# Local softmax of every other head pair: the shift and the sums on VectorE, one ScalarE exponential of 640 columns, and a new order table

## The chip, the core and the metric

The kernel runs on one core of a Trainium2 chip. The core has five engines that run side by side, each with its own queue of instructions in order: TensorE (PE in the profile; its weight loads are PEld), VectorE (DVE), ScalarE (ACT), GpSimd (POOL) and SyncE (SP), which issues the DMAs. The metric is the device time of one execution, in microseconds, as the median of several runs.

## What is computed

Inputs are q, k, v (4 batches, 8 heads, 576 positions, 64 columns) and the weights of two mixing layers. The first part is the one the change is about:

```python
# local attention: |i - j| < 4; 1/sqrt(64) = 0.125
scores = np.where(mask, scale * np.matmul(q, k.transpose(0, 1, 3, 2)), -1000000000.0)
scores = scores - np.max(scores, axis=-1, keepdims=True)
attn = np.exp(scores)
attn = attn / (np.sum(attn, axis=-1, keepdims=True) + 1e-09)
out = out_up + np.matmul(attn, v)     # out_up: attention over means of 4 positions
```

Then a token mixer (576 to 256 to 576 positions), a channel mixer (512 to 1536 to 512 columns, both with ReLU and a residual), and an attention layer with four experts of which each token uses two.

## The kernel before

*Units.* A unit is one pair of heads of one batch: 4 batches x 4 pairs = 16 units, numbered 0 to 15. For the local attention the 576 positions are cut into ten windows of 58 queries that see 64 keys each. A unit's scores are a PSUM tile `sl` of 128 partitions by 2 x 5 x 64 = 640 columns: two windows above each other, five pairs of windows (`t`), two heads (`h`). The mask is added by a first product of a band with an identity matrix.

*Steps of a unit.* `q` loads queries and keys, `sl` makes the scores (PE), `mx` takes the maximum over 64 keys with a minus sign into `nraw` (VectorE) and scales it by 0.125 into `nmx`, `ex` makes ten exponentials of 64 columns, each with its bias from `nmx` and with its row sum (ScalarE; the sum is read by an instruction of its own), `rs` adds 1e-9 and inverts (VectorE), `P` multiplies (GpSimd), `tl` transposes (PE), `tc` copies out of PSUM (ScalarE). The steps `qd kd sd md ed rd Pd pdt pc` do the same for the down-sampled attention, `v` and `pv` bring the values. For two units at a time `ol` multiplies with the values, `oc` copies the down-sampled part and `ad` adds both into `u` (VectorE).

*The token mixer* runs by halves of a batch: `tx` transposes, `xh` and `xl` split into a high and a low part (ScalarE, VectorE), `h` is the first product, `hh` and `hl` split its ReLU, `pu` is the second product and `ua` adds it to `u` (VectorE). *Weights* 0 to 12 come as 64-bit numbers and are turned by `w g t a f gd add hi lo` over SP, ScalarE, VectorE and GpSimd. *The channel mixer* begins with the steps `uh ul` (split of `u`), `fc` (first product), `gh gl`, `sc` (second product) and `ac`, and goes on in a loop, `ch_step`, behind the table. The expert layer follows in a second written table, which the change leaves alone.

*What sets the order.* In the attention stage the order of all steps is written out by hand in the table `STEPS`: each engine gets its instructions in the order of the words and carries them out in that order. PSUM has four single banks and two double banks there (`ABANKS`); `sl` and `sd` share the two double ones. `P` has four buffers, `nraw`, `nmx`, `sm` and `rs` three.

Of the kernel before, what the change touches and what calls it, by code (L numbers as in the profile page):

```python
# [49 lines left out]
STEPS = """  # L50
    w0 q0 g0 t0 w1 qd0 q1 g1 sl0 kd0 gd0 a0 mx0 gd1 sd0 f0 q2 ex0 add0 a1 kd1 t1 sl1 q3 md0 qd1 f1 add1 ed0 rs0 kd2
    hi0 hi1 w2 mx1 ex1 qd2 sd1 rd0 lo0 g2 md1 lo1 ed1 P0 tl0.0 sd2 tc0.0 qd3 v0 rs1 w3 t2 sl2 kd3 Pd0 P1 md2 rd1
    pdt0 g3 gd2 a2 ed2 mx2 rd2 f2 tl1.0 q4 tl0.1 v1 add2 gd3 t3 pc0 q5 sd3 ex2 tl1.1 Pd1 qd4 md3 pdt1 hi2 a3 tc0.1
    lo2 rs2 ed3 w4 rd3 pv0 q6 Pd2 tc1.0 pc1 tc1.1 sl3 g4 mx3 pv1 ex3 f3 sl4 v2 gd4 a4 t4 w5 mx4 qd5 v3 f4 rs3 ol0.0
    ol0.1 sl5 Pd3 add3 P2 kd4 P3 oc0 add4 ex4 ad0.3 ad0.0 ad0.1 pdt3 ad0.2 pc3 mx5 tx0.1 tl3.0 xh0.1 pv2 tx0.2 rs4
    tc3.0 xl0.1 q7 sd4 w6 xh0.2 hi4 hi3 tx0.0 pv3 kd5 xh0.0 tl2.0 xl0.2 md4 tl2.1 xl0.0 lo3 tl3.1 P4 tc2.0 h0.0 lo4
    qd7 ex5 g6 pdt2 pc2 h0.1 rs5 sd5 g5 gd5 ed4 gd6 a6 a5 f5 md5 tc3.1 t6 f6 sl7 tc2.1 v4 hh0 t5 ed5 ol1.0 kd7 hl0
    oc1 add5 mx7 rd4 hi5 ol1.1 ad1.0 add6 hi6 lo5 ex7 ad1.1 sl6 ad1.3 v5 pu0.0 q8 ad1.2 ua0.0 tl4.0 tx1.2 tc4.0 lo6
    xh1.2 kd6 mx6 pv5 q9 w7 P5 xl1.2 kd9 tx1.1 q10 xh1.1 pu0.1 pu0.2 Pd4 rd5 xl1.1 ua0.1 ua0.2 pu0.3 tl5.0 Pd5 ex6
    pdt4 tx1.0 xh1.0 w8 qd6 ua0.3 pv4 qd9 tc5.0 sd7 kd10 pc4 sd6 qd8 tl5.1 xl1.0 v6 kd8 rs6 md7 g7 pdt5 tl4.1 g8 pc5  # L60
    tc4.1 ed7 tc5.1 P6 t7 h1.0 gd7 h1.1 rs7 t8 v7 md6 gd8 a7 hh1 sl9 f7 hl1 ol2.0 ed6 mx9 rd7 oc2 ex9 ol2.1 q11
    ad2.0 sd9 ad2.1 pv6 pu1.0 ad2.3 w9 v8 rd6 Pd7 ad2.2 pdt7 tx2.1 sl8 pu1.1 md9 q12 ua1.0 ed9 q13 pc7 rs9 xh2.1
    qd10 q14 pu1.2 mx8 ua1.1 pv7 pu1.3 ex8 xl2.1 Pd6 a8 rd9 ua1.2 tx2.0 ua1.3 pdt6 tx2.2 xh2.0 tl6.0 pc6 sd8 xh2.2
    tc6.0 P9 f8 P7 sd10 rs8 xl2.0 tl6.1 tl7.0 xl2.2 md10 tc6.1 qd11 tc7.0 tl9.0 md8 v9 P8 qd12 qd13 tl8.0 tc9.0
    tc8.0 ed8 tl9.1 add8 tl7.1 qd14 h2.0 add7 ed10 tc9.1 tc7.1 h2.1 sl10 ol3.0 hh2 Pd9 pv8 v10 kd11 oc3 mx10 hl2 rd8
    ad3.0 hi7 ex10 pv9 Pd8 sl11 ol3.1 pu2.0 ad3.2 ad3.1 ad3.3 ua2.0 mx11 pu2.1 tx3.2 pdt8 tx3.1 xh3.2 ua2.1 xl3.2
    tx3.0 pdt9 pc8 lo7 xh3.1 xh3.0 xl3.1 tl8.1 sd11 xl3.0 ex11 kd12 pu2.2 md11 kd14 h3.0 tc8.1 pc9 rs10 g9 ua2.2
    sd12 ed11 pu2.3 P10 rs11 P11 md12 ed12 h3.1 gd9 a9 f9 rd12 hh3 ol4.0 hl3 oc4 t9 ua2.3 sl13 ad4.0 v11 ad4.1 sl12
    tl10.0 pv10 rd10 add9 tl11.0 v12 w10 tc10.0 mx12 tc11.0 q15 ol4.1 rd11 ad4.2 pu3.0 Pd10 ua3.0 pu3.1 tl11.1 ex12
    ad4.3 tx4.0 tc11.1 xh4.0 ua3.1 tx4.2 pu3.2 tx4.1 mx13 xh4.2 xl4.0 pv12 xl4.2 pdt10 tl10.1 ua3.2 hi8 xh4.1 hi9  # L70
    kd13 w11 ex13 xl4.1 lo9 rs12 lo8 pu3.3 h4.0 g10 pv11 h4.1 tc10.1 rs13 pc10 sd13 hh4 P12 ua3.3 tl12.0 hl4 Pd11
    md13 pdt11 tl12.1 g11 pc11 gd11 tc12.0 a11 pu4.0 gd10 v13 tc12.1 ua4.0 ed13 qd15 ol5.0 sl14 kd15 oc5 P13 a10
    ol5.1 ad5.0 t10 sl15 ad5.1 tl13.0 tc13.0 ad5.2 ad5.3 rd13 mx15 tx5.2 tx5.0 tx5.1 xh5.2 xh5.0 pu4.1 Pd13 xl5.2
    xl5.0 xh5.1 xl5.1 ex15 tl13.1 mx14 pu4.2 ua4.1 f10 ua4.2 tc13.1 pv13 add10 Pd12 h5.0 pu4.3 h5.1 ex14 pdt12 pdt13
    hh5 sd15 sd14 rs15 ua4.3 hl5 pu5.0 rs14 pc13 pc12 P14 ol6.0 P15 hi10 md15 f11 md14 ua5.0 oc6 ed15 pu5.1 pu5.2
    ad6.0 ad6.1 ol6.1 lo10 ua5.1 rd15 w12 v14 ua5.2 ed14 t11 ad6.3 Pd15 g12 pu5.3 tl14.0 rd14 ad6.2 tx6.2 v15 ua5.3
    Pd14 tx6.0 gd12 tc14.0 tl14.1 tx6.1 xh6.2 xh6.0 xh6.1 tc14.1 xl6.2 xl6.0 xl6.1 tl15.0 pdt14 tc15.0 pdt15 t12
    pv14 pv15 a12 tl15.1 pc15 h6.0 tc15.1 h6.1 pc14 hh6 f12 ol7.0 hl6 oc7 ol7.1 ad7.1 ad7.0 ad7.2 pu6.0 ad7.3 uh0.3
    uh0.2 ul0.2 uh0.1 ua6.0 add12 tx7.1 tx7.2 uh0.0 tx7.0 ul0.1 ul0.0 xh7.0 hi12 ul0.3 xh7.2 pu6.1 fc0.0 fc0.1 xh7.1
    gh0.0 add11 xl7.0 xl7.1 gl0.0 fc0.2 hi11 pu6.2 gh0.1 gh0.2 uh1.3 gl0.1 ua6.1 xl7.2 gl0.2 h7.0 lo11 pu6.3 uh1.0  # L80
    uh1.2 lo12 sc0.2 ul1.3 ul1.2 uh1.1 h7.1 ul1.0 uh2.1 ac0.2 sc0.3 ul1.1 ua6.2 fc1.0 ac0.3 gh1.0 gl1.0 sc0.0 hh7
    hl7 fc1.1 ac0.0 gh1.1 ul2.1 fc1.2 gl1.1 pu7.0 pu7.1 pu7.2 uh2.2 gh1.2 sc0.1 gl1.2 ua6.3 uh2.3 ul2.3 ul2.2 ua7.2
    uh2.0 ua7.1 ul2.0 pu7.3 ac0.1 ua7.0 ua7.3
"""


# [958 lines left out]
```

## Time and profile before

| | |
|---|---|
| median of 3 runs | 659.18 us (659.09 to 660.15) |
| the profiled execution | 660.12 us, span 658.3 us |
| busy: PE, PEld | 627.7, 562.6 us |
| busy: VectorE, ScalarE, GpSimd | 443.1, 378.6, 148.3 us |
| mean granted TensorE clock | 0.99 of full speed |

The span runs from the first to the last instruction. Busy time is the union of an engine's instructions; PE's products are pipelined, so a busy PE is not a PE at its peak. The attention stage takes about the first 150 us; the first channel product starts at 152.81 us.

### The profile page before, as it was taken

The numbers are of one execution on the slowest core, as the hardware profiler recorded it, in microseconds if no ns is written. First come the engines' busy times: TensorE is split into PE (matmuls) and PEld (weight loads), VectorE is DVE, ScalarE is ACT, GpSimd is POOL, SyncE is SP. The second block draws the span as 40 slices with busy tenths as digits, with TensorE's granted clock in tenths as the row PEclk, the third lists the DMA queues.
The fourth block names the chain that finished last, engine by engine and source line by source line (L and its number), as shares of the span: only waits on it lengthen the run. The fifth ranks groups of instructions, "written<-read, shape, count | busy, mean of one in ns | idle before, by whom it ended". The sixth has DMA issues, their size and how long they took to land.

```text
span 658.3 us, 13779 instructions
## 1 busy us (share of the span) xinstructions
PE 627.7 (95%) x5196; PEld 562.6 (85%) x5196; DVE 443.1 (67%) x1075; ACT 378.6 (58%) x1213; POOL 148.3 (23%) x167
## 2 busy tenths in 40 slices
PE   3888999999999999999999999999989999999996
...
DVE  7889977787688767447644545443488766858871
ACT  6988999865364544234433332320387787677782
...
DMA packets 28947, 46.78 MB, mean 71 GB/s; under 512 B 3216, under 2 KB 16016, under 8 KB 28880
## 3 DMA queue, kind: packets, MB, share of 16 engines
...
## 4 chain that ended last, share of the span: by engine, by line
PE 80%; ACT 9%; DVE 7%; DMA 2%; issue 1%; SPq 0%; ACTq 0%; DVEq 0%
PE c L218 46%; PE proj L218 7%; PE vp L218 4%; PE wo L218 4%; PE o L943 4%; ACT P L411 4%; PE pt L920 3%; PE s L881 2%; PE s L882 2%; PE pu L218 2%; ACT pd L440 2%; PE h L218 2%; DMA wt_raw<-in_wt_dram 1%; DVE u L521 1%; PE tl L468 1%
## 5 line engine op out<-in xcount | busy, mean ns | idle before, releaser
L218 PE MATMUL c<-uh,wch 128*128 128x460 f32 (+1 forms) x240 | 89.2, 372 | 0.0
L218 PE MATMUL c<-hh,wch 128*128 128x460 f32 (+1 forms) x240 | 89.2, 371 | 0.0
L218 PE MATMUL c<-hl,wch 128*128 128x460 f32 (+1 forms) x240 | 89.1, 371 | 0.0
L218 PE MATMUL c<-hh,wcl 128*128 128x460 f32 (+1 forms) x240 | 89.1, 371 | 0.0
L218 PE MATMUL c<-ul,wch 128*128 128x460 f32 (+1 forms) x240 | 89.1, 371 | 0.0
L218 PE MATMUL c<-uh,wcl 128*128 128x460 f32 (+1 forms) x240 | 88.9, 371 | 0.0
L198 ACT ACTIVATE hh<-c 128x460 fp32r<-128x460 f32 (+1 forms) x60 | 33.0, 550 | 90.4 <-PE c L218 90.1
L776 POOL TENSOR_TENSOR vlo<-u,vh 128x576 fp32r<-128x576 f32 x16 | 22.8, 1425 | 240.2 <-ACT vh L772 240.2
L207 DVE SCALAR_TENSOR_TENSOR hl<-c,hh 128x460 fp32r<-128x460 f32 (+1 forms) x60 | 38.1, 635 | 55.2 <-ACT hh L198 55.0
L280 POOL TENSOR_TENSOR wc_t<-wc_f,wc_t 128x512 int32<-128x512 int32 x24 | 31.8, 1336 | 157.6 <-ACT wc_t L269 137.8
L638 ACT ACTIVATE uh<-u 128x460 fp32r<-128x460 f32 (+1 forms) x80 | 45.3, 585 | 25.0 <-PE c L218 19.8
L644 DVE TENSOR_TENSOR ul<-u,uh 128x460 fp32r<-128x460 f32 (+1 forms) x80 | 51.9, 664 | 8.3 <-ACT uh L638 8.3
L898 ACT ACTIVATE Pc<-Pc,nm 116x116 f32<-116x116 f32 (+4 forms) x80 | 46.7, 586 | 8.1 <-DVE nm L891 6.1
L891 DVE CUSTOM_DVE_ANT_0 Pc<-s,caus 116x348 f32<-116x348 f32 (+4 forms) x80 | 40.2, 515 | 15.2 <-PE s L882 11.6
L218 PEld LDWEIGHTS c<-hh,wcl 128*128 128x128 f32 x240 | 45.1, 188 | 5.3
L218 PEld LDWEIGHTS c<-uh,wcl 128*128 128x128 f32 x240 | 45.1, 188 | 5.2
L218 PEld LDWEIGHTS c<-hh,wch 128*128 128x128 f32 x240 | 45.2, 188 | 5.1
L218 PEld LDWEIGHTS c<-ul,wch 128*128 128x128 f32 x240 | 45.1, 188 | 5.1
L218 PEld LDWEIGHTS c<-uh,wch 128*128 128x128 f32 x240 | 45.1, 188 | 5.1
L218 PEld LDWEIGHTS c<-hl,wch 128*128 128x128 f32 x240 | 45.1, 188 | 5.1
L411 ACT ACTIVATE P<-sl,nmx 128x64 f32<-128x64 f32 x160 | 47.9, 355 | 2.7 <-DVE nmx L404 2.7
L411 ACT ACTIVATION_READ_ACCUMULATOR P<-sl,nmx 128x1 f32 x160 | 38.8, 249 | 0.0
...
## 6 DMA issues: line engine op xcount, KB each, us to landing
...
```

The source lines that it names most:

```text
L198: nc.scalar.activation(hi, src, AF.Relu if relu else AF.Copy, **({"scale": scale} if scale else {}))
L207: nc.vector.scalar_tensor_tensor(lo, src, 0.0, h, op0=OP.max, op1=OP.subtract)
L218: mm(ps, a, c, start=first and i == 0, stop=last and i == n - 1)
L280: nc.gpsimd.tensor_tensor(t, r["f"], t, op=OP.add)
L411: nc.scalar.activation(P[:, t, h], r["sl"][:, h, t], AF.Exp, bias=r["nmx"][:, t, h:h + 1], scale=0.125, accum_out=sm[:, 2 * t + h:2 * t + ...
L638: nc.scalar.activation(hi, UA[:, c, blocks[k]], AF.Copy)
L644: nc.vector.tensor_tensor(lo, UA[:, c, blocks[k]], hi.bitcast(F32), op=OP.subtract)
L776: nc.gpsimd.tensor_tensor(lo, U[b][:, c], hi.bitcast(F32), op=OP.subtract)
L891: nc.vector.tensor_tensor_reduce(dst, r["s", t, e], mask, -1.0, 3.0e38, OP.add, OP.min, nm[:nq])
L898: nc.scalar.activation(P[:nq, :n], P[:nq, :n], AF.Exp, bias=r["nm", t, e][:nq], scale=-1.0, accum_out=r["su", t][:nq, e:e + 1])
L920: tp(pt[:TS[c], (c - c0) * TQ:(c - c0) * TQ + nq], P[:nq, c * TQ:c * TQ + TS[c]], ident[:nq, :nq])
L943: mm(o[64 * e:64 * e + 64, a - q0:q1 - q0], BR[b]["VV"][:TS[c], c, ec:ec + 64], PT[e][:TS[c], column(c, a):column(c, a) + q1 - a], start=( ...
```

## The change

In units 0, 2, ..., 14 (`WHOLE`) the step `mx` ends with the maximum, without the scaling to `nmx`. A new step `sb` adds the negated maximum to all 640 scores out of PSUM into `P` (VectorE, the maximum broadcast over 64 columns). `ex` is then one exponential of 640 columns in place, in SBUF, with the scale 0.125 and no bias and no sums. A new step `sm` sums 64 columns each of `P` (VectorE). The odd units stay as they were. The table is written anew: the old steps are all there, the 16 new ones added, in another order. The diff, the table cut to the lines spoken of later:

```diff
@@ -47,40 +47,41 @@
 QB = 5
 
 NU, NH = B * NP, 2 * B
+WHOLE = range(0, NU, 2)
 STEPS = """
-    w0 q0 g0 t0 w1 qd0 q1 g1 sl0 kd0 gd0 a0 mx0 gd1 sd0 f0 q2 ex0 add0 a1 kd1 t1 sl1 q3 md0 qd1 f1 add1 ed0 rs0 kd2
...
-    ol5.1 ad5.0 t10 sl15 ad5.1 tl13.0 tc13.0 ad5.2 ad5.3 rd13 mx15 tx5.2 tx5.0 tx5.1 xh5.2 xh5.0 pu4.1 Pd13 xl5.2
-    xl5.0 xh5.1 xl5.1 ex15 tl13.1 mx14 pu4.2 ua4.1 f10 ua4.2 tc13.1 pv13 add10 Pd12 h5.0 pu4.3 h5.1 ex14 pdt12 pdt13
-    hh5 sd15 sd14 rs15 ua4.3 hl5 pu5.0 rs14 pc13 pc12 P14 ol6.0 P15 hi10 md15 f11 md14 ua5.0 oc6 ed15 pu5.1 pu5.2
-    ad6.0 ad6.1 ol6.1 lo10 ua5.1 rd15 w12 v14 ua5.2 ed14 t11 ad6.3 Pd15 g12 pu5.3 tl14.0 rd14 ad6.2 tx6.2 v15 ua5.3
-    Pd14 tx6.0 gd12 tc14.0 tl14.1 tx6.1 xh6.2 xh6.0 xh6.1 tc14.1 xl6.2 xl6.0 xl6.1 tl15.0 pdt14 tc15.0 pdt15 t12
-    pv14 pv15 a12 tl15.1 pc15 h6.0 tc15.1 h6.1 pc14 hh6 f12 ol7.0 hl6 oc7 ol7.1 ad7.1 ad7.0 ad7.2 pu6.0 ad7.3 uh0.3
-    uh0.2 ul0.2 uh0.1 ua6.0 add12 tx7.1 tx7.2 uh0.0 tx7.0 ul0.1 ul0.0 xh7.0 hi12 ul0.3 xh7.2 pu6.1 fc0.0 fc0.1 xh7.1
...
+    q0 sl0 q1 qd0 mx0 kd0 kd1 w0 g0 t0 w1 qd1 sd1 sb0 gd0 a0 ex0 sl1 f0 q2 g1 md1 sm0 mx1 ed1 gd1 rd1 q3 a1 rs0 add0
+    sl2 hi0 ex1 qd2 kd2 w2 f1 t1 mx2 sd0 sb2 lo0 g2 sl3 Pd1 pdt1 md0 q4 qd4 gd2 rs1 v0 a2 P0 t2 kd3 ex2 add1 ed0 kd4
...
+    sl13 ex12 qd12 ed11 mx13 ad4.1 ol4.1 lo7 h3.0 ad4.3 sm12 ad4.2 pu2.3 ua2.3 rd11 qd14 ex13 pv11 h3.1 tl11.1 tx4.1
+    hh3 pv10 sd13 xh4.1 sd12 kd14 hl3 xl4.1 tc11.1 pu3.0 tx4.2 Pd11 g9 Pd10 pdt11 gd9 xh4.2 pc11 ua3.0 v12 pdt10
+    tx4.0 a9 pc10 xl4.2 tl10.1 xh4.0 tc10.1 hi8 pu3.1 pu3.2 v13 xl4.0 h4.0 md12 pv13 pu3.3 h4.1 md13 ua3.2 qd15
+    ua3.1 ol5.0 ed13 pv12 rd13 lo8 sl15 ua3.3 rs13 ed12 hh4 oc5 f9 hl4 P13 ol5.1 sl14 Pd13 kd15 ad5.0 rd12 mx15 rs12
+    pu4.0 g10 ad5.2 ad5.1 mx14 pu4.1 ad5.3 tl13.0 tx5.2 ua4.0 tx5.1 t9 ex15 tc13.0 xh5.2 ua4.1 sb14 xh5.1 P12 v14
+    xl5.2 tx5.0 Pd12 add9 pu4.2 xl5.1 hi9 xh5.0 sd14 ex14 t10 v15 w11 sd15 tl13.1 pdt13 ua4.2 xl5.0 md15 tl12.0 lo9
+    pdt12 tc13.1 gd10 sm14 pc13 tl12.1 tc12.0 tc12.1 h5.0 pu4.3 rs15 g11 rs14 h5.1 ed15 gd11 pv15 md14 ua4.3 rd15
...
+    tx7.0 tx7.1 uh0.0 uh0.1 hi10 uh0.3 ul0.1 tx7.2 h6.1 uh0.2 ul0.3 ul0.2 uh1.3 ul0.0 fc0.0 hh6 lo10 xh7.0 gh0.0 g12
+    hl6 t11 xh7.1 f11 pu6.0 fc0.1 xh7.2 ul1.3 gl0.0 t12 gh0.1 fc0.2 xl7.1 add11 gd12 xl7.2 uh1.1 uh2.3 a12 xl7.0 f12
+    uh1.2 pu6.1 gl0.1 hi11 ul2.3 gh0.2 add12 lo11 gl0.2 uh1.0 ua6.1 h7.0 hi12 pu6.2 lo12 ua6.2 ul1.0 h7.1 ul1.2
+    sc0.3 sc0.0 ua6.0 pu6.3 hh7 ul1.1 ac0.3 fc1.0 ac0.0 hl7 fc1.1 ua6.3 gh1.0 gh1.1 gl1.0 pu7.0 fc1.2 gh1.2 pu7.1
...
 
@@ -400,10 +401,27 @@
         def local_max():
             raw = pa.tile([128, 2 * NT], F32, tag="nraw", bufs=3, name="nraw")
             nc.vector.tensor_reduce(raw.rearrange("p (t h) -> p h t", h=2), r["sl"], axis=AX.X, op=OP.max, negate=True)
+            r["raw_max"] = raw
+            if i in WHOLE:
+                return
             r["nmx"] = pa.tile([128, NT, 3], F32, tag="nmx", bufs=3, name="nmx")
             nc.vector.tensor_scalar_mul(r["nmx"][:, :, :2], raw.rearrange("p (t h) -> p t h", h=2), 0.125)
 
+        def local_shift():
+            P = r["P"] = pa.tile([128, NT, 2, WIN], F32, tag="P", bufs=4, name=f"P{b}_{p}")
+            nc.vector.tensor_tensor(P.rearrange("p t h k -> p h t k"), r["sl"],
+                                    r["raw_max"].rearrange("p (t h) -> p h t", h=2)[:, :, :, None].to_broadcast([128, 2, NT, WIN]),
+                                    op=OP.add)
+
+        def local_total():
+            r["sm"] = pa.tile([128, 2 * NT], F32, tag="sm", bufs=3, name="sm")
+            nc.vector.tensor_reduce(r["sm"], r["P"].rearrange("p t h k -> p (t h) k"), axis=AX.X, op=OP.add)
+
         def local_exp():
+            if i in WHOLE:
+                P = r["P"].rearrange("p t h k -> p (t h k)")
+                nc.scalar.activation(P, P, AF.Exp, scale=0.125)
+                return
             P = r["P"] = pa.tile([128, NT, 2, WIN], F32, tag="P", bufs=4, name=f"P{b}_{p}")
             sm = r["sm"] = pa.tile([128, 2 * NT], F32, tag="sm", bufs=3, name="sm")
             for t in range(NT):
@@ -473,7 +491,8 @@
             t0, t1 = ((0, 3), (3, 5))[part]
             nc.scalar.activation(r["PT"][:, t0:t1].rearrange("p t q -> p (t q)"), r["tl", part][:, :(t1 - t0) * 128], AF.Copy)
 
-        steps = dict(q=load_qk, v=load_v, qd=pool_q, kd=pool_k, pv=pool_v, sl=local, mx=local_max, ex=local_exp,
+        steps = dict(q=load_qk, v=load_v, qd=pool_q, kd=pool_k, pv=pool_v, sl=local, mx=local_max, ex=local_exp, sb=local_shift,
+                     sm=local_total,
                      rs=local_sum, P=local_norm, sd=down, md=down_max, ed=down_exp, rd=down_sum, Pd=down_norm, pdt=turn_down,
                      pc=keep_down, tl=turn, tc=keep)
         return steps, r
```

## Rows read from the trace of the kernel before

**Rows 1.** The page: three lines of its 40 slices (busy tenths).

```profile
PE   3888999999999999999999999999989999999996
...
DVE  7889977787688767447644545443488766858871
ACT  6988999865364544234433332320387787677782
```

**Rows 2.** Stretches: from, to, length, busy us of each engine, clock, DMA share, GB/s.

```profile
0.00:10.00 10.00, 3.39 (x52) 2.45 (x53) 6.08 (x14) 4.32 (x13) 5.03 (x21) 1.00 0.78 277
...
49.00:86.00 37.00, 34.63 (x611) 31.29 (x606) 33.71 (x79) 33.32 (x162) 28.24 (x33) 0.95 0.66 202
...
50.00:60.00 10.00, 8.10 (x156) 7.11 (x148) 9.53 (x21) 8.77 (x52) 9.07 (x12) 0.92 0.62 198
...
116.60:132.30 15.70, 14.44 (x292) 13.57 (x291) 11.26 (x30) 12.36 (x61) 5.56 (x6) 1.00 0.31 87
...
132.30:153.00 20.70, 17.91 (x310) 15.78 (x310) 18.92 (x39) 13.76 (x41) 10.63 (x10) 1.00 0.26 75
...
153.00:184.00 31.00, 31.00 (x174) 28.62 (x174) 20.75 (x38) 13.40 (x26) 2.83 (x2) 1.00 0.10 35
...
0.00:153.00 153.00, 130.45 (x2273) 116.08 (x2274) 127.15 (x295) 127.89 (x587) 101.15 (x129) 0.98 0.56 172
```

**Rows 3.** Chain that ended last, shares by line: 0 to 153, then 153 to 184.

```profile
by line: ACT P L411 15.3%; ACT pd L440 7.7%; PE h L218 5.7%; PE pu L218 4.8%; DMA wt_raw<-in_wt_dram 3.9%; issue 3.8%; DVE u L521 3.7%; PE tl L468 3.6%; PE tx L537 3.5%; ACT PT L474 3.1%; PE sl L396 3.0%; PE sd L426 2.8%; DVE u L580 2.5%; D
...
by line: PE c L218 74.2%; PE pu L218 15.5%; PE h L218 9.2%; PE h L560 1.5%
```

**Rows 4.** Waits from 0 to 153: engine, line, releaser, us in total, times, longest.

```profile
DVE h1l L207 <- ACT h1h L198: 4.2, 3, 2.4
...
PE sl L389 <- ACT P L411: 3.6, 2, 3.3
...
DVE nraw L402 <- PE sl L396: 3.4, 4, 1.4
```

**Rows 5.** Chain in order of time, two pieces: start us, us, what.

```profile
63.49 1.14 ACT wc_g L267 x2
...
123.92 2.96 ACT P L411 x20
```

**Rows 6.** ScalarE's groups, 0 to 200: count, busy us, mean ns, idle time before.

```profile
L474 ACT ACTIVATE PT<-tl 128x384 f32<-128x384 f32 x16 | 7.7, 502 | 3.9 <-PE tl L468 3.9
...
L474 ACT ACTIVATE PT<-tl 128x256 f32<-128x256 f32 x16 | 6.4, 410 | 0.2 <-PE tl L468 0.2
```

**Rows 7.** VectorE's groups, 0 to 200: count, busy us, mean ns, idle time before.

```profile
L580 DVE TENSOR_TENSOR u<-pu,u 128x288 f32<-128x288 f32 x32 | 13.9, 444 | 0.9 <-PE pu L218 0.9
...
L402 DVE TENSOR_REDUCE nraw<-sl 128x10 f32<-128x640 f32 x16 | 13.0, 816 | 3.5 <-PE sl L396 3.4
...
L211 DVE TENSOR_TENSOR xl<-tx,xh 128x512 fp32r<-128x512 f32 x16 | 10.7, 686 | 2.0 <-ACT xh L198 1.8
...
L274 DVE SCALAR_TENSOR_TENSOR wc_f<-wc_raw,wc_a 128x512 int32<-128x512 int32 x12 | 10.3, 856 | 1.5 <-POOL wc_t L280 1.2
...
L211 DVE TENSOR_TENSOR wcl<-wc_t,wch 128x512 fp32r<-128x512 f32 x11 | 8.8, 816 | 1.7 <-ACT wch L198 1.7
...
L271 DVE TENSOR_SCALAR wc_a<-wc_g 128x512 int32<-128x512 int32 x12 | 7.3, 611 | 0.2
...
L277 DVE TENSOR_SCALAR wc_g<-wc_g 128x512 f32<-128x512 f32 x12 | 6.9, 576 | 0.7 <-ACT wc_g L267 0.7
...
L404 DVE TENSOR_SCALAR nmx<-nraw 128x10 f32<-128x10 f32 x16 | 2.6, 165 | 0.5
...
L211 DVE TENSOR_TENSOR wt_0l<-wt_t,wt_0h 128x512 fp32r<-128x512 f32 x1 | 1.6, 1598 | 0.0
```

**Rows 8.** VectorE's timeline near 110: start us, duration us, instruction.

```profile
109.53 0.68 DVE L211 TENSOR_TENSOR xl<-tx,xh 128x512 fp32r<-128x512 f32 x1
110.13 0.68 DVE L211 TENSOR_TENSOR wcl<-wc_t,wch 128x512 fp32r<-128x512 f32 x1
```

More of the change, by code (lines that the diff above doesn't have):

```diff
@@ L49 @@
 NU, NH = B * NP, 2 * B
+WHOLE = range(0, NU, 2)
 STEPS = """
-    w0 q0 g0 t0 w1 qd0 q1 g1 sl0 kd0 gd0 a0 mx0 gd1 sd0 f0 q2 ex0 add0 a1 kd1 t1 sl1 q3 md0 qd1 f1 add1 ed0 rs0 kd2
-    hi0 hi1 w2 mx1 ex1 qd2 sd1 rd0 lo0 g2 md1 lo1 ed1 P0 tl0.0 sd2 tc0.0 qd3 v0 rs1 w3 t2 sl2 kd3 Pd0 P1 md2 rd1
-    pdt0 g3 gd2 a2 ed2 mx2 rd2 f2 tl1.0 q4 tl0.1 v1 add2 gd3 t3 pc0 q5 sd3 ex2 tl1.1 Pd1 qd4 md3 pdt1 hi2 a3 tc0.1
-    lo2 rs2 ed3 w4 rd3 pv0 q6 Pd2 tc1.0 pc1 tc1.1 sl3 g4 mx3 pv1 ex3 f3 sl4 v2 gd4 a4 t4 w5 mx4 qd5 v3 f4 rs3 ol0.0
@@ L55 @@
[L55 to L69, printed above, removed]
@@ L70 @@
-    ad4.3 tx4.0 tc11.1 xh4.0 ua3.1 tx4.2 pu3.2 tx4.1 mx13 xh4.2 xl4.0 pv12 xl4.2 pdt10 tl10.1 ua3.2 hi8 xh4.1 hi9
-    kd13 w11 ex13 xl4.1 lo9 rs12 lo8 pu3.3 h4.0 g10 pv11 h4.1 tc10.1 rs13 pc10 sd13 hh4 P12 ua3.3 tl12.0 hl4 Pd11
-    md13 pdt11 tl12.1 g11 pc11 gd11 tc12.0 a11 pu4.0 gd10 v13 tc12.1 ua4.0 ed13 qd15 ol5.0 sl14 kd15 oc5 P13 a10
-    ol5.1 ad5.0 t10 sl15 ad5.1 tl13.0 tc13.0 ad5.2 ad5.3 rd13 mx15 tx5.2 tx5.0 tx5.1 xh5.2 xh5.0 pu4.1 Pd13 xl5.2
-    xl5.0 xh5.1 xl5.1 ex15 tl13.1 mx14 pu4.2 ua4.1 f10 ua4.2 tc13.1 pv13 add10 Pd12 h5.0 pu4.3 h5.1 ex14 pdt12 pdt13
@@ L80 @@
[L80 to L83, printed above, removed]
+    q0 sl0 q1 qd0 mx0 kd0 kd1 w0 g0 t0 w1 qd1 sd1 sb0 gd0 a0 ex0 sl1 f0 q2 g1 md1 sm0 mx1 ed1 gd1 rd1 q3 a1 rs0 add0
@@ new lines @@
+    sl2 hi0 ex1 qd2 kd2 w2 f1 t1 mx2 sd0 sb2 lo0 g2 sl3 Pd1 pdt1 md0 q4 qd4 gd2 rs1 v0 a2 P0 t2 kd3 ex2 add1 ed0 kd4
+    mx3 P1 pc1 w3 rd0 sl4 f2 hi1 Pd0 ex3 tl0.0 tl0.1 sm2 tc0.0 add2 v1 tl1.0 pdt0 q5 lo1 pv0 w4 hi2 pv1 g3 tl1.1 mx4
+    sd2 qd3 sb4 rs2 lo2 pc0 tc1.0 ex4 rs3 sd3 gd3 q6 md2 tc1.1 a3 tc0.1 P3 md3 t3 g4 ed2 gd4 ol0.0 a4 ol0.1 f3 f4
+    kd5 oc0 ed3 sd4 ad0.0 add3 t4 ad0.3 ad0.2 ad0.1 tl3.0 md4 P2 tx0.1 rd3 hi3 add4 lo3 tc3.0 xh0.1 tx0.0 tx0.2
+    tl3.1 xh0.0 v2 q7 xh0.2 ed4 Pd3 xl0.1 xl0.0 sl5 xl0.2 pdt3 pv2 tl2.0 sl6 rd2 sm4 hi4 tc3.1 w5 Pd2 kd6 mx5 tc2.0
```

16 lines of the change are left out of this document (added).

## The prediction

> **What bounds the kernel now.** I read the page's 40 slices first [rows 1]. PE is at eight or nine tenths from the third slice to the end; VectorE (DVE) and ScalarE (ACT) are high in the first nine slices, some 150 us, and far lower behind them. So the kernel has two regimes, and the change touches only the first, the attention stage that the written table orders.
>
> The second view is the table of stretches [rows 2]. I cut it where PE begins the value products of a pair (49.0, 86.0, 116.6, 132.3), and where the first channel products begin (153). From 153 on PE is busy all the time, and the chain that ended last there is nothing but PE's products [rows 3]: behind that point the end comes as much earlier as PE gets there earlier. Up to 153 it is otherwise: PE 130.45 us, DVE 127.15, ACT 127.89 busy of 153. Three engines carry almost the same load and each stands still for 22 to 26 us. No single one is the bound. The chain before 153 says the same: local exponentials are its largest line with 15.3%, but down-sampled exponentials, PE products and VectorE additions share the rest [rows 3].
>
> The third view is the waits up to 153 [rows 4]. VectorE's longest idle time is listed behind ScalarE (the low half of the hidden layer, 4.2), the next behind PE (local maxima, 3.4), and PE in turn waited 3.6 us for the local exponentials, because these read the score banks to the last column and only two double banks exist.
>
> **The change part by part.**
>
> *ScalarE.* A unit's ten exponentials with their ten sum reads are one run of 20 instructions on the chain, 2.96 us [rows 5]. They overlap; the run is the price. In eight units one exponential of 640 columns takes its place. The nearest rows are ScalarE passes SBUF to SBUF of 512 columns, two of which took 1.14 us, so 0.57 each [rows 5], and the copies of 384 and 256 columns out of PSUM, 502 and 410 ns, so 0.09 us for 128 more columns [rows 6]. I take 0.57 + 0.09 = 0.66 us. Bounds: 0.57, and 0.71 (the 0.57 scaled by 640/512). ACT is relieved of 8 x (2.96 - 0.66) = 18.4 us.
>
> *VectorE.* The maximum over the scores stays (816 ns) [rows 7]. The small scaling to `nmx` goes in eight units (165 ns). New is the subtraction, one PSUM and one broadcast SBUF operand, 640 columns. Nearest are the additions of 288 columns out of PSUM, 444 ns, and the 512-column subtraction out of PSUM, 686 ns: 1.08 ns a column, so 0.82 us at 640. New too is the sum over 640 columns: the same reduction as the maximum, 0.82 us, now from SBUF. Neighbours start before the one ahead is recorded as done (a 512-column one starts at 109.53, the next at 110.13, 0.60 later at 0.68 duration) [rows 8], so one of the two costs 0.74. Together 0.74 + 0.82 - 0.165 = 1.40 us a unit, 11.2 us in eight. Bounds: 9.9 (both at 640 x 1.08 ns, nothing fixed) and 24 (both at 1.6 us). The upper one comes from one weight's split of 512 columns that took 1598 ns, against 686 for the transposed split of as many [rows 7]; all 16 maxima average 816 ns, and the new pair is nearest to these, so I take the short value. The `P` tile of such a unit is claimed at the subtraction, not at the exponential; of four buffers I expect no wait.
>
> The Trainium skill ("SBUF — State Buffer", section "Who interferes with whom") says that VectorE and GpSimd lock each other out only where the VectorE instruction reads two SBUF inputs or runs in a two-port mode. By that rule neither new instruction stretches; if both did by as much as the weight splits (816 against 686 ns in the mean, a fifth), the load below would be 136.0 in place of 133.5 us and the gain 1.8 in place of 4.5. The trace agrees as far as it goes: the stretched rows have two SBUF inputs, the maxima none.
>
> *The table.* Between it and the first channel product (`fc0.0`) the new table leaves out `a12 f11 f12 gd12 lo10 hl6 ua6.0` for VectorE, which now come behind it: 0.61 + 2 x 0.86 + 0.58 + 0.82 + 0.69 (as the split of as many columns) + 0.44 = 4.9 us [rows 7], of which I count 4.8 for the overlap. ScalarE's moved steps (`g12 t11 t12 hi12 hh6`, two `xh7`, less one `uh`) are six, net, of some 0.6 us: 3.6. On SP's queue the first weight load is moved behind two query and key pairs, four DMAs: the first scores can start one issue earlier, the first weight lands four issues later, and its conversion fills ScalarE's and VectorE's first microseconds less well. I cost that at nothing, since the weight's user, the first token product, stands far down the table; without that cover it is the delay of four issues, once. PE and GpSimd do the same work.
>
> *The sum up to the first channel product.* VectorE: 127.15 + 11.2 - 4.8 = 133.5 us. ScalarE: 127.9 - 18.4 - 3.6 = 105.9. So VectorE alone becomes the limit, ScalarE gets 47 us of room, and the question is how densely VectorE runs. Of its first 10 us it was busy 6.08 [rows 2], waiting for the first data, which stays. Behind them remain 133.5 - 6.1 = 127.4 us of work. Density now over 10 to 153: (127.15 - 6.08)/143 = 84.7%. Break-even is 127.4/143 = 89.1%.
>
> How dense can it get? Where VectorE is the engine that others wait for, it ran at 33.71/37.0 = 91.1% (49 to 86) and 18.92/20.7 = 91.4% (132.3 to 153); in the best piece that I looked at, 50 to 60, 95% [rows 2]. The order speaks for the dense end. In the old table ScalarE's work between a unit's maximum and its sum exceeds VectorE's: for unit 15, between `mx15` and `rs15`, ScalarE has two whole local exponentials (5.9 us) and more, VectorE some 4 us, so VectorE runs dry. In the new one, for unit 14 between `sb14` and `sm14`, VectorE has about 4.1 us and ScalarE 3.1, for unit 13 between `mx13` and `rs13` 12.6 against 8.8 (steps counted at the rows' durations; in units 2 and 8 it is the other way, 5.2 against 6.8 and 15.8 against 19.0). And a score bank of an even unit is free after the subtraction, some 1.6 us after its scores (a maximum and a subtraction), no longer after a run of 2.96 us more: PE's 3.6 us of waiting shrinks. What queues behind a late sum is every `u` addition and `xl` split, and PE's transposes behind them; this is the danger.
>
> I take 92%, a little over the two rows where VectorE set the pace, since the listed waits behind ScalarE are the ones that go: 127.4/0.92 + 10 = 148.5 us in place of 153, a gain of 4.5. The profiled execution's own time is 660.12 us, 0.94 over the median of the three runs; 660.12 - 4.5 = 655.6, which against the median is **654.7 us**. At 95% it would be 144.1, a gain of 8.9.
>
> **The rivals.**
>
> *Faster by some microseconds (the forecast, densities from 90 to 95%): 650 to 658.* For it: ScalarE's room and the spaced-out sums. Against it: VectorE's queue holds small things others need, and nothing can pass in it.
>
> *Slower: VectorE's in-order queue becomes the bound at the density it has now.* Place: the attention stage, `sb` and `sm` ahead of the `u` additions and `xl` splits. At 84.7% the first channel product would start at 127.4/0.847 + 10 = 160.4, 7.4 us later: 666.6. It decides as soon as density stays under 89.1%. For it: from 116.6 to 132.3 VectorE was busy only 11.26 of 15.7 us [rows 2], and an even unit's way from scores to sum now holds three long VectorE instructions in place of one, any of which can be stuck behind something late. Against it: the longest listed idle time is behind ScalarE.
>
> *No change: the gain is given back behind the first channel product.* The 4.8 us that were moved fall into 153 to 184, where VectorE was busy 20.75 of 31 us [rows 2]; with them it would be 25.6, 82%, with the last three token halves and three weights to deliver in order. If PE waits there for as long as it came early: 659.2. Against it: channel products of blocks that are split already can fill in.
>
> *ScalarE was the bound after all.* Half of the exponentials' 23.4 us on the chain (15.3% of 153), times 2.30/2.96, gives 9.1 us: 650.1. Against it: its load was no higher than VectorE's.
>
> **How the numbers follow.** The repeats lie within 1.1 us, so 0.2%, 1.3 us, is about what can be told from no change. Forecast (gain of 1.3 to 8.9): 0.52; ScalarE as the bound, more than that: 0.07; no change, by giving back or by densities of 88 to 90%: 0.15; slower: 0.26. That is 0.59 faster, 0.15 same, 0.26 slower. Bounds of the new costs move the sum by -1.3 us at the low end; the stretched end, 12.8 us, is part of the slower case and unlikely. Range 649.5 to 663.0: it leaves out some 0.06 below and 0.13 above. The faster case alone spans 650 to 658.
>
> **What will show it.** ScalarE's local exponentials: 80 of 64 columns left and 8 of 640 at about 0.75 us recorded; its total near 360 us in place of 378.6. VectorE's total near 454 in place of 443.1, eight subtractions and eight sums near 0.82 us each. The first channel product near 148.5 in place of 153, VectorE over 90% between 10 us and there, with ScalarE no longer among its releasers and PE's wait for local exponentials under 2 us. PE without a gap behind the first channel product. The prediction is wrong if VectorE stays below 89%, if the new instructions stretch beside GpSimd, or if PE has new gaps between the first channel product and 184.

## The result and the profile after

The changed kernel takes **644.89 us** (median of 4 runs, 643.72 to 645.35) against 659.23 before (4 runs beside them): ratio 0.9777, 95% interval 0.976 to 0.9794. Predicted were 654.7 us and 649.5 to 663.0; the measured time lies 4.6 us below that range. The direction was right, the size was not: a gain of 14.3 us in place of 4.5. The profiled execution took 644.59 us, with a span of 642.5 us.

The slices of the page, to set beside [rows 1]; the last line is TensorE's granted clock in tenths:

```profile
PE   4789999999999999999999999999989999999997
...
DVE  7999998779696876467644554443497766857871
ACT  4898977765464453343422332420488777777783
...
PEclk9999999999999999999999999999999999999999
```

ScalarE's row falls early, VectorE's stays high for nine slices. The stretches, with the columns of [rows 2], are cut where the first channel product starts:

```profile
0.00:10.00 10.00, 3.55 (x56) 2.50 (x60) 5.63 (x12) 2.56 (x4) 6.00 (x23) 1.00 0.80 267
10.00:138.32 128.32, 117.12 (x2208) 105.50 (x2205) 117.00 (x280) 104.69 (x425) 93.08 (x104) 1.00 0.58 176
0.00:138.32 138.32, 120.67 (x2260) 107.99 (x2261) 122.63 (x291) 107.25 (x428) 99.08 (x127) 1.00 0.60 183
138.32:642.50 504.18, 497.31 (x2938) 446.62 (x2936) 320.93 (x792) 254.23 (x633) 50.38 (x40) 1.00 0.15 43
```

The first channel product starts at 138.32 us, before at 152.81: 14.5 us earlier, nearly all of the 15.8 us between the two profiled spans. What follows it took 504.2 us, before 658.3 - 152.81 = 505.5. Nothing was given back behind it; there the chain holds PE's products alone, as in [rows 3]. The two chains, 0 to 138.32 and 138.32 to 170:

```profile
by line: PE pu L219 13.6%; PE h L219 13.2%; DMA wt_raw<-in_wt_dram 4.4%; PE tx L556 4.3%; PE sd L444 4.1%; DVE nraw L403 3.8%; PE tl L486 3.7%; PE olx L531 3.7%; DVE ndraw L450 3.5%; issue 3.0%; PE olx L522 2.9%; DVE wt_f L275 2.7%; PE sl L
...
by line: PE c L219 71.7%; PE pu L219 17.5%; PE h L219 9.1%; PE h L579 2.3%
```

The local exponentials, 15.3% of the stage's chain in [rows 3], are gone from the listed part; PE's token products lead. The waits of [rows 4] that were spoken of, up to 138.32:

```profile
PE sl L390 <- ACT pd L458: 3.5, 2, 2.2
...
PE sd L444 <- ACT P L429: 2.2, 2, 1.9
DVE h1l L208 <- ACT h1h L199: 1.9, 2, 1.5
DVE nraw L403 <- PE sl L397: 1.5, 1, 1.5
```

VectorE's two longest listed waits halved (4.2 to 1.9, 3.4 to 1.5). No wait of the scores `sl` for a local exponential is listed any more; the down-sampled scores, which share their banks, still wait for one. The new instructions and what is left of the old, up to 138.32 (columns of [rows 7]):

```profile
L429 ACT ACTIVATE P<-sl,nmx 128x64 f32<-128x64 f32 x80 | 23.8, 332 | 1.0 <-DVE nmx L408 0.6 <-DVE rs L434 0.4
...
L412 DVE TENSOR_TENSOR P<-sl,nraw 128x640 f32<-128x640 f32 x8 | 6.5, 813 | 0.1
...
L418 DVE TENSOR_REDUCE sm<-P 128x10 f32<-128x640 f32 x8 | 6.4, 798 | 0.0
L423 ACT ACTIVATE P<-P 128x640 f32<-128x640 f32 x8 | 6.0, 746 | 0.2 <-DVE P L412 0.2
...
L408 DVE TENSOR_SCALAR nmx<-nraw 128x10 f32<-128x10 f32 x8 | 1.3, 165 | 0.3
```

**Where VectorE's load went.** It was about 127.0 us up to the first channel product (127.15 up to 153 in [rows 2]); 133.5 were predicted, and it is 122.63. The pair of new instructions less the scaling is 6.5 + 6.4 - 1.3 = 11.6, as predicted (11.2). The rest went down by some 16 us, where I had counted 4.8. Groups of before, up to 152.81:

```profile
L274 DVE SCALAR_TENSOR_TENSOR wc_f<-wc_raw,wc_a 128x512 int32<-128x512 int32 x8 | 7.5, 940 | 1.3 <-POOL wc_t L280 1.2
L277 DVE TENSOR_SCALAR wc_g<-wc_g 128x512 f32<-128x512 f32 x8 | 5.2, 653 | 0.3 <-ACT wc_g L267 0.3
L271 DVE TENSOR_SCALAR wc_a<-wc_g 128x512 int32<-128x512 int32 x8 | 5.1, 635 | 0.1
...
L277 DVE TENSOR_SCALAR wt_g<-wt_g 128x288 f32<-128x288 f32 x4 | 4.0, 1032 | 0.7 <-ACT wt_g L267 0.7
```

and of after, up to 138.32:

```profile
L278 DVE TENSOR_SCALAR wc_g<-wc_g 128x512 f32<-128x512 f32 x5 | 3.1, 612 | 0.1
L275 DVE SCALAR_TENSOR_TENSOR wc_f<-wc_raw,wc_a 128x512 int32<-128x512 int32 x4 | 3.0, 740 | 0.0
L272 DVE TENSOR_SCALAR wc_a<-wc_g 128x512 int32<-128x512 int32 x5 | 2.9, 575 | 0.0
...
L278 DVE TENSOR_SCALAR wt_g<-wt_g 128x288 f32<-128x288 f32 x4 | 1.3, 317 | 0.0
```

The three `wc` groups fell from 17.8 to 9.0 us. Ten of their instructions went behind the first channel product, where the table names four (`f11 f12 a12 gd12`). The other six belong to two weights of the *next* group, which stand in no table: they come from the loop behind it, and the framework that builds the instruction streams had placed them ahead of the first splits of `u` in the kernel before; now they stand behind the first channel product. So the sentence ahead of the prediction, that each engine gets its instructions in the order of the words, holds for the table's steps alone. At the after rows' means those six are 2 x (740 + 612 + 575) = 3.9 us.

The other part is shorter instructions. The four `wt_g` of 288 columns fell from 4.0 to 1.3 us, four splits of 288 columns from 5.3 to 1.7 (the longest took 2633 ns before, 395 after); in the other direction two 512-column `wt_f` rose by 1.1 and two 512-column splits by 1.4. With the smaller ones the 28 VectorE instructions of the token weights sum to 15.8 us in place of 20.7 (counts times mean durations), 4.9 us less. The new table does this, not the new form: the same 28 sum to 15.9 us in the run table_only and to 21.2 in form_only below. The largest of them, in the timelines of GpSimd and VectorE, before:

```profile
29.73 1.36 POOL L451 TENSOR_TENSOR pd<-pd,rd 72x576 f32<-72x576 f32 x1
31.06 0.79 POOL L280 TENSOR_TENSOR wt_t<-wt_f,wt_t 128x288 int32<-128x288 int32 x1
31.81 1.26 POOL L420 TENSOR_TENSOR P<-P,rs 128x640 f32<-128x640 f32 x1
33.03 0.73 POOL L375 TENSOR_TENSOR pool<-kT 128x288 f32<-128x288 f32 x1
...
30.02 3.22 DVE L277 TENSOR_SCALAR wt_g<-wt_g 128x288 f32<-128x288 f32 x1
```

and after:

```profile
28.94 0.59 POOL L383 TENSOR_TENSOR vd<-vr 112x192 f32<-112x192 f32 x1
30.28 1.26 POOL L438 TENSOR_TENSOR P<-P,rs 128x640 f32<-128x640 f32 x1 [0.74 <-ACT PT L492]
...
30.05 0.25 DVE L278 TENSOR_SCALAR wt_g<-wt_g 128x288 f32<-128x288 f32 x1
```

The same operation took 3.22 us while GpSimd ran its instructions without a break, and 0.25 us in the 0.74 us in which GpSimd stood still. The Trainium skill ("SBUF — State Buffer", section "Who interferes with whom") lists the `tensor_scalar` among the VectorE operations that can take the pair of ports shared with GpSimd, and says that whoever is second is blocked for the whole of the other's instruction; these rows agree in kind, but the wait here lasts over three instructions of GpSimd and not over one.

### The profile page after: what moved, and what is told of

Same layout as the page of the kernel before. It is cut to its first block, busy times and chain, and to the rows that moved or that the text cites. A ratio compares the mean times of both kernels' runs of the same rounds, so it can differ in the third digit from the quotient of the medians.

```text
span 642.5 us, 13638 instructions
## 1 busy us (share of the span) xinstructions
PE 618.0 (96%) x5196; PEld 554.6 (86%) x5196; DVE 443.6 (69%) x1083; ACT 361.5 (56%) x1061; POOL 149.5 (23%) x167
## 4 chain that ended last, share of the span: by engine, by line
PE 87%; DVE 9%; DMA 1%; issue 1%; ACT 1%; POOL 1%; SPq 0%; ACTq 0%; DVEq 0%; POOLq 0%
PE c L219 47%; PE proj L219 7%; PE vp L219 4%; PE wo L219 4%; PE pu L219 4%; PE o L962 4%; PE pt L939 3%; PE h L219 3%; PE s L900 2%; PE s L901 2%; DMA wt_raw<-in_wt_dram 1%; PE tx L556 1%; PE sd L444 1%; DVE nraw L403 1%; PE tl L486 1%
## 5 line engine op out<-in xcount | busy, mean ns | idle before, releaser
L939 PE MATMUL pt<-ident,Pc 116*116 116x116 f32 (+2 forms) x240 | 35.2, 263 | 2.9 <-DVE Pc L928 2.6
L928 DVE TENSOR_SCALAR Pc<-Pc,su,gw 116x464 f32<-116x464 f32 (+4 forms) x80 | 36.3, 478 | 0.7
```

The source lines that it names most:

```text
L928: nc.vector.tensor_scalar(P[:nq, :n], P[:nq, :n], r["su", t][:nq, e:e + 1], BR[b]["w"][:nq, t, 2 * p + e:2 * p + e + 1], op0=OP.mult, op1= ...
L939: tp(pt[:TS[c], (c - c0) * TQ:(c - c0) * TQ + nq], P[:nq, c * TQ:c * TQ + TS[c]], ident[:nq, :nq])
```

## The experiments

Each kernel was timed beside the kernel before, whose median was 658.71 us beside the first four, 659.40 beside the next four and 659.24 beside the last two. "Over the changed kernel" means over its 644.89 us, which were measured beside 659.23; the medians of the kernel before differ by up to 0.7 us from set to set. The windows run from 0 or 10 us to the first channel product, with the columns of [rows 2].

**table_only: the new table with the old form.**

```diff
-WHOLE = range(0, NU, 2)
+WHOLE = ()
...
         def local_shift():
+            if i not in WHOLE:
+                return
...
         def local_total():
+            if i not in WHOLE:
+                return
```

> The new table with all 16 units in the old form (the 16 new steps issue nothing). Theory A, ScalarE's load: the gain of 14 us comes from the 18.4 us taken off ScalarE, which lets VectorE and PE run on; without it the time goes back to 655 to 662 us. Theory B, the order: the new table alone, with its later weight conversions and wider gaps, brings the gain; 645 to 650 us. Theory C, both are needed together: 652 to 657.

Measured: **687.13 us**, ratio 1.0427 (1.0394 to 1.046). The windows, the chain, two waits and the `wt_g` row up to the first channel product at 179.56:

```profile
0.00:179.56 179.56, 132.26 (x2260) 119.31 (x2261) 116.29 (x283) 125.89 (x580) 98.62 (x127) 0.90 0.46 141
10.00:179.56 169.56, 128.80 (x2208) 116.84 (x2208) 111.33 (x272) 123.42 (x578) 92.64 (x104) 0.90 0.44 133
...
by line: ACT P L433 21.3%; PE h L219 10.7%; PE pu L219 9.6%; PE sd L448 4.3%; ACT pd L462 4.1%; PE olx L526 4.0%; PE sl L397 3.9%; DMA wt_raw<-in_wt_dram 3.5%; PE olx L535 3.3%; PE tl L490 2.9%; PE pdt L480 2.8%; PE tx L560 2.7%; issue 2.2%
...
PE sl L390 <- ACT P L433: 17.5, 5, 4.3
...
PE sd L448 <- ACT P L433: 16.7, 6, 3.9
...
L278 DVE TENSOR_SCALAR wt_g<-wt_g 128x288 f32<-128x288 f32 x4 | 1.3, 320 | 0.0
```

That lies outside the ranges of all three theories. Up to the first channel product VectorE has 6.3 us less to do than in the changed kernel (116.29 against 122.63), and this product comes 41 us later: in this order PE waits 34 us for the local exponentials, which lead the chain with 21.3%. The table alone brings nothing; it fits the new form.

**form_only: the old table, with `sb` right behind `mx` and `sm` right ahead of `rs` in the even units.**

```diff
-    w0 q0 g0 t0 w1 qd0 q1 g1 sl0 kd0 gd0 a0 mx0 gd1 sd0 f0 q2 ex0 add0 a1 kd1 t1 sl1 q3 md0 qd1 f1 add1 ed0 rs0 kd2
+    w0 q0 g0 t0 w1 qd0 q1 g1 sl0 kd0 gd0 a0 mx0 sb0 gd1 sd0 f0 q2 ex0 add0 a1 kd1 t1 sl1 q3 md0 qd1 f1 add1 ed0 sm0
+    rs0 kd2
...
```

> The old table with the new form in the even units, the subtraction right behind each maximum and the sum right before each inversion. Theory A: 645 to 651 us, most of the gain. Theory B: no gain, 657 to 662, or slower, since VectorE gets 11.5 us more in an order that was not made for it. Theory C: 652 to 657.

Measured: **662.82 us**, 1.0055 (1.0037 to 1.0073).

```profile
0.00:159.84 159.84, 132.12 (x2272) 116.41 (x2273) 139.83 (x303) 111.61 (x435) 101.07 (x129) 0.95 0.53 165
10.00:159.84 149.84, 128.48 (x2220) 113.94 (x2217) 134.23 (x292) 108.17 (x431) 96.06 (x108) 0.94 0.52 158
...
L278 DVE TENSOR_SCALAR wt_g<-wt_g 128x288 f32<-128x288 f32 x4 | 4.6, 1170 | 0.7 <-ACT wt_g L268 0.7
```

VectorE 134.23 of 149.84 is 89.6%, with 139.8 us in all up to there. The form alone is the rival that ends slower, as theory B had it. Form alone costs 4.1 us and the table alone 28.4; together they gain 14.3.

**scalar_back: the changed kernel with ScalarE's relief given back**, as eight copies of 240 constant columns behind each long exponential.

```diff
                 nc.scalar.activation(P, P, AF.Exp, scale=0.125)
+                for _ in range(8):
+                    nc.scalar.activation(extra, caus[:, :240], AF.Copy)
```

> The changed kernel with eight copies of 240 columns behind each of the eight long exponentials, which nobody waits for: about 2.3 us a unit, so ScalarE's old load of 18.4 us is back while banks are freed as early as in the changed kernel. Theory A: 655 us or more. Theory B: under 648 us. If what counts is not the load but that the score banks come free earlier: under 650 us as well, and then the table-only kernel tells the two apart.

Measured: **668.24 us**, 1.0133 (1.0103 to 1.0162), 23 us over the changed kernel, for these copies:

```profile
L426 ACT ACTIVATE extra<-caus 128x240 f32<-128x240 f32 x64 | 25.9, 404 | 1.8
```

The copies took 404 ns each, where I had reckoned with some 290, so more was given back than the change had taken: ScalarE's total rose by 23.9 us, to 385.4, and the first channel product came at 159.94. ScalarE's load is then 130.94 up to there, 82%, and lumps of it cost almost one for one. Theory A's range holds; whether load or lumps cost the time, this run doesn't tell.

**vector_more: the changed kernel with two sums over a constant ahead of each new sum.**

```diff
         def local_total():
+            for _ in range(2):
+                nc.vector.tensor_reduce(extra, caus[:, :576].rearrange("p (g r) -> p g r", r=4), axis=AX.X, op=OP.add)
```

> The changed kernel with two sums over 576 columns of a constant tile ahead of each of the eight new sums, which nobody waits for: some 0.7 us each, 11.5 us more on VectorE. If VectorE is the bound of the changed kernel's attention stage, as the prediction had it: 10 us or more are lost, 655 us. If PE is (the chain there is mostly PE): under 4 us are lost, at most 649 us.

Measured: **657.93 us**, 0.9977 (0.9959 to 0.9996).

```profile
10.00:150.23 140.23, 123.06 (x2208) 110.23 (x2202) 128.68 (x297) 105.59 (x426) 92.31 (x104) 0.99 0.52 160
...
L419 DVE TENSOR_REDUCE extra<-caus 128x144 f32<-128x576 f32 x16 | 11.9, 742 | 0.3
```

11.9 us more on VectorE cost 13.0. With them VectorE's load up to the first channel product is 134.0 us, almost the 133.5 that I had predicted, and this product starts at 150.23, 1.7 us behind the predicted 148.5. At that load the prediction's way to this point holds within 1.7 us; of the gain of 4.5 us that it forecast, 0.8 is left against the kernel before (658.71).

**form_late_weights: form_only with the conversions of the two weights from behind the table held back** until the first second product of the channel mixer (a copy out of its result into their raw tile, overwritten by the load).

```diff
+            if name in ("wc1_3", "wc1_4"):
+                nc.vector.tensor_copy(raw[:, 0:1, 0].bitcast(F32), ACC[:, 0, 0:1])
```

> The old table with the new form, in which two weights of the next group (wc1_3, wc1_4) are loaded and turned only after the first second product, in place of before the first channel product. That takes 2 x (0.94 + 0.59 + 0.84) = 4.7 us off VectorE ahead of the first channel product. If VectorE's load there counts one for one: 658 us, 4 to 5 less than the form alone (662.8). If these conversions only filled holes: 661.5 to 663.5.

Measured: **661.8 us**, 1.0041 (1.0026 to 1.0056), 1.0 under form_only's median, with overlapping intervals, and inside the range that was set for conversions which only filled holes.

```profile
0.00:155.15 155.15, 130.93 (x2272) 115.07 (x2273) 135.47 (x296) 110.63 (x433) 101.01 (x129) 0.96 0.54 163
```

In the profile VectorE had 4.4 us less to do and the first channel product came 4.7 us earlier (155.15), but the span was only 3.3 shorter (659.4 against 662.7), and form_only's profiled execution was its longest (664.65). So in the old order the move saves between nothing and 3 us: this run does not settle its worth.

**scalar_spread: the changed kernel with 64 such copies on ScalarE, one behind each `tc` and `pc` and one ahead of each `ed`.**

```diff
+    def fill():
+        nc.scalar.activation(extra, caus[:, :240], AF.Copy)
...
+            fill()
```

> The changed kernel with 64 copies of 240 columns on ScalarE, one behind each copy out of PSUM of the two attentions and one ahead of each down-sampled set of exponentials: the load of the kernel with eight copies behind each long exponential, but spread. If ScalarE's load counts wherever it stands: 662 us or more. If ScalarE has room and only the lump of 2.3 us ahead of waiting steps cost time: 645 to 652.

Measured: **655.43 us**, 0.9931 (0.9911 to 0.995), 10.5 over the changed kernel for 16.4 us of ScalarE (total 377.9 in place of 361.5). That is between the two ranges: some two thirds of the load cost time, and the rest found room. VectorE's density fell to 118.43/137.77 = 86.0%:

```profile
10.00:147.77 137.77, 121.00 (x2201) 107.19 (x2193) 118.43 (x280) 121.05 (x489) 92.63 (x104) 0.99 0.53 163
```

**warm: the kernel before with the band products of units 0 to 5 made four times.**

```diff
+            for n in range(4 if i < 6 else 1):
...
-                       band[hs, None, :].to_broadcast([64, NT, WIN]), start=True, stop=False)
+                           band[hs, None, :].to_broadcast([64, NT, WIN]), start=True, stop=i < 6 and n < 3)
```

> The kernel before with the band products of units 0 to 5 made four times (three times for nothing), some 5 us more on PE in the first 60 us, where it stood still for 14 us. TensorE's granted clock was 0.90 to 0.95 from 30 to 70 us in the kernel before and 1.00 in the changed one. If that clock is part of the 14 us: a clock nearer to 1.00 and 656 to 658 us, at most 3 less than before. If it follows from the waits and costs nothing: 659 to 662.

Measured: **661.25 us**, 1.0024 (1.0006 to 1.0041); the stage's mean clock was 0.98, as before.

```profile
30.00:70.00 40.00, 32.83 (x604) 28.99 (x606) 34.90 (x74) 35.54 (x170) 31.02 (x39) 0.91 0.68 205
```

From 30 to 70 us, too, the mean was 0.91 as in the kernel before. The products did not raise it, so this shows nothing of what the clock's step from 0.98 to 1.00 in the changed kernel is worth.

**qd_pool: the changed kernel with `qd` of units 8 to 15 on GpSimd, in two additions.**

```diff
+            if i >= 8:
+                q4 = r["q"].rearrange("p (g r) -> p g r", r=4)
+                a = pa.tile([128, SD, 2], F32, tag="pool2", bufs=2, name="pool2")
+                nc.gpsimd.tensor_tensor(a, q4[:, :, 0:2], q4[:, :, 2:4], op=OP.add)
+                nc.gpsimd.tensor_tensor(r["qd"], a[:, :, 0], a[:, :, 1], op=OP.add)
+                return
```

> The changed kernel with the pooling of the queries of units 8 to 15 made by GpSimd in two additions (1.1 us) in place of VectorE's reduction (0.74 us): 5.9 us off VectorE, 9 us more on GpSimd, which was busy 99 of 138 us. If VectorE's load counts one for one: 639 to 641 us. If GpSimd's queue, which these additions now share with the normalisations, is as tight: 644 to 650.

Measured: **651.56 us**, 0.9874 (0.9854 to 0.9895), 6.7 over the changed kernel and above both ranges.

```profile
0.00:144.32 144.32, 122.47 (x2260) 110.80 (x2261) 119.91 (x283) 107.55 (x428) 107.46 (x143) 0.98 0.58 175
...
L212 DVE TENSOR_TENSOR wcl<-wc_t,wch 128x512 fp32r<-128x512 f32 x4 | 3.5, 883 | 0.0
```

The eight reductions take 5.9 us off VectorE, but its load up to the first channel product, now at 144.32, fell by 2.7 only: weight instructions ran longer again (these splits 883 ns in place of 674). GpSimd's load rose by 8.4.

**vector_late: seven such sums between the last pair's additions in the changed kernel.**

```diff
+            if k == 7:
+                for _ in range(2 if x < 3 else 1):
+                    nc.vector.tensor_reduce(extra, caus[:, :576].rearrange("p (g r) -> p g r", r=4), axis=AX.X, op=OP.add)
```

> The changed kernel with seven sums over a constant (742 ns each in an earlier run, 5.2 us in all; they change nothing) between the additions of the last pair, some 3 to 6 us ahead of the first channel product. VectorE has about that much work less there than I had counted from the table. If VectorE's load counts one for one at this place too, the first channel product comes at about 143.5 in place of 138.3 and the time is near 650. Rival: the last microseconds before the first channel product have holes that take such work in (VectorE stood still for some 4 us of the last ten); then the loss stays under 2 us and the time at or below 646.5, and conversions that moved away from there cannot explain the gain.

Measured: **650.19 us**, 0.9865 (0.9844 to 0.9886), 5.3 over the changed kernel for 5.2 us:

```profile
10.00:142.38 132.38, 122.66 (x2211) 110.29 (x2209) 121.91 (x287) 104.82 (x426) 93.07 (x104) 0.99 0.55 171
...
L546 DVE TENSOR_REDUCE extra<-caus 128x144 f32<-128x576 f32 x7 | 5.2, 748 | 0.1
```

The first channel product came 4.1 us later, and what follows it took 1.4 longer. Load at this late place counts about one for one in the time too; the holes did not take it in.

**conversions_back: the changed kernel's table with ten steps (eight of the weights, `hh6`, `hl6`) moved ahead of `fc0.0`.**

```diff
-    tx7.0 tx7.1 uh0.0 uh0.1 hi10 uh0.3 ul0.1 tx7.2 h6.1 uh0.2 ul0.3 ul0.2 uh1.3 ul0.0 fc0.0 hh6 lo10 xh7.0 gh0.0 g12
-    hl6 t11 xh7.1 f11 pu6.0 fc0.1 xh7.2 ul1.3 gl0.0 t12 gh0.1 fc0.2 xl7.1 add11 gd12 xl7.2 uh1.1 uh2.3 a12 xl7.0 f12
+    tx7.0 tx7.1 g12 uh0.0 t11 uh0.1 hi10 gd12 f11 uh0.3 ul0.1 tx7.2 h6.1 t12 hh6 uh0.2 lo10 a12 ul0.3 hl6 f12 ul0.2 uh1.3 ul0.0 fc0.0 xh7.0 gh0.0
+    xh7.1 pu6.0 fc0.1 xh7.2 ul1.3 gl0.0 gh0.1 fc0.2 xl7.1 add11 xl7.2 uh1.1 uh2.3 xl7.0
```

> The changed kernel with nine conversion steps (g12 t11 t12 gd12 f11 a12 f12 lo10 and hh6 hl6) moved back from behind the first channel product to ahead of it, among the last pair's additions and splits; no work is added. VectorE gets some 4 us more ahead of the first channel product and as much less behind it, ScalarE some 2.4. If the move was worth what its load counts, the first channel product comes 4 to 5 us later and the time is near 649. Rival: what is moved ahead is saved again behind it, where PE then waits less, and the time stays within 1.5 us of the changed kernel's.

Measured: **658.08 us**, 0.9979 (0.9966 to 0.9993), 13.2 over the changed kernel: three times what the higher of the two expectations allowed. VectorE's timeline and pieces of the chain show why:

```profile
136.68 0.43 DVE L278 TENSOR_SCALAR wc_g<-wc_g 128x512 f32<-128x512 f32 x1 [2.39 <-ACT wc_g L268]
...
131.96 3.94 DMA wc_raw<-in_wc_dram
...
135.98 0.16 ACT wc_g L268
...
137.00 0.48 ACT uh L657
```

`g12` at its new place heads ScalarE's queue before its weight has landed, and the splits of `u` (`uh`) stand behind it. The first channel product came 5.9 us later and what follows took 7.6 longer. So this run prices a stall and not the load.

## Why the prediction was wrong

The step that failed is the sum "VectorE: 127.15 + 11.2 - 4.8 = 133.5 us" up to the first channel product; it measured 122.6. The term 4.8, what leaves VectorE ahead of that product, was mis-sized: about 16 us left. 8.8 of them are in the three `wc` groups (2.7 named in the table, 3.9 two weights that it does not name, some 2 shorter instructions), 4.9 are shorter instructions of the token weights, and the rest is in `h1l` and in neighbours that overlap more. The sum compared the words of two tables at fixed prices; it left out what the loop behind the table adds and that the same instructions could become shorter. With 122.63 - 5.63 = 117.0 us behind 10 us and the predicted 92%, the same formula gives 117.0/0.92 + 10 = 137.2; measured were 138.3.

- *ScalarE, 18.4 us less*: right within 1.3 us. The long exponential took 746 ns (predicted about 750), ScalarE's load up to the first channel product was 107.3 us (105.9), its total 361.5 (360), 17.1 less.
- *The prices of the new VectorE instructions*: right, 813 and 798 ns in the mean (820 each), the longest 825 and 810, so nothing stretched. The Trainium skill's rule (same page and section) that I weighed there agrees. I applied it to the two new instructions only. It also bears on those that a new table *shifts* against GpSimd's work, and the 4.9 us of shorter weight instructions are such ones as far as the timelines show. The lower bound of the new work, 9.9 us, is 9.7 by its own terms, which changes nothing.
- *The density*: 117.00/128.32 = 91.2%, predicted 92%.
- *VectorE as the sole limit, "47 us of room" on ScalarE*: half right. In the changed kernel VectorE's added work costs 1.1 and 1.0 us per us, all over the stage and just ahead of its end (vector_more, vector_late). But little of ScalarE's room was there: the same order lost 23 us for 24 in lumps and 10.5 for 16.4 spread out, and 6.7 with 8.4 us more on GpSimd, though VectorE was relieved there. That ScalarE stands still for 22% of the stage and GpSimd for 28% was for the most part not free time. I put that down to the queues, which are in order: added work delays whatever stands behind it and is waited for.
- *First weight load moved behind two query and key pairs*: costed at nothing. VectorE's first 10 us held 5.63 us of work (6.08 before); no run took this alone.
- *Nothing given back behind the first channel product*: right, 504.2 us against 505.5.
- *The signs*: ScalarE is still among VectorE's releasers (1.9 us in `h1l`), and PE still waited 2.2 us for a local exponential, at the down-sampled scores.
- *The rivals.* "Slower" is what the form does in the old table (662.82; 666.6 was worked out for a density of 84.7%, it had 89.6%). "ScalarE the bound after all" came nearest in time (650.1), and table_only shows ScalarE's exponentials as the leading line of that chain, so its relief is a condition of the gain in the new order; form_only shows that the relief alone brings nothing. "No change" fell.
- *VectorE's total near 454*: measured 443.6, against 443.1 before. Over the whole span shorter weight instructions cancel 9.1 of the added 11.6 us (4.9 in the token weights, 4.3 in the `wc` groups and splits); most of the rest is overlap.

Shown by runs: the gain needs both parts; load added to VectorE counts about one for one in the new order, at the late place too; with the load that I had predicted, the first channel product comes within 1.7 us of the forecast. Read from the traces and not tried alone: that the token weights' 4.9 us come from the shift against GpSimd's work and are worth as much, and the moved conversions theirs; the two runs on the latter came out at 1.0 us within their spread and at a stall. Open too is TensorE's part. Its granted clock was 0.98 in this stage before and 1.00 after, which is its upper level (2.4 GHz) throughout, and PE's busy time up to the first channel product fell from 130.45 us [rows 2] to 120.67 on almost the same products; no run tells whether that follows from shorter waits or is a part of the cause. In vector_more, where the load is back, it was 126.7 at a clock of 0.99.
